# Recurrence outputs made turned by their products, and one chunk's first product moved ahead

## The chip, the cores and the metric

The kernel runs on one core of a Trainium2 chip. The metric is device time in microseconds (us) of one execution, as a median of several runs. The core has five engines that work side by side, each through its own queue in order: TensorE (PE; its weight loads are listed as PEld), VectorE (DVE), ScalarE (ACT), GpSimd (POOL), and SyncE (SP), which issues most of the transfers between device memory and the on-chip memory. TensorE writes into PSUM, eight banks of 512 words in each of 128 rows; ScalarE and VectorE read it from there.

## The reference

Two blocks follow each other. The first is a delta rule recurrence over 768 time steps for 4 batches of 8 heads of width 48, the second a gated feed-forward block over the 3072 tokens with 384 features, inner width 1536. All is in 32 bits.

```python
k_n = k / (norm(k) + 1e-6)
state = zeros((B, H, D, D))
for t in range(S):
    y[:, :, t] = einsum('bhd,bhde->bhe', q[:, :, t], state)
    v_old = einsum('bhde,bhd->bhe', state, k_n[:, :, t])
    state = state + beta[:, :, t] * einsum('bhd,bhe->bhde', k_n[:, :, t], v[:, :, t] - v_old)
x = y.transpose(0, 2, 1, 3).reshape(B * S, H * D)
g, val = x @ w_gate, x @ w_val
out = (g * sigmoid(g) * val) @ w_out
```

## The kernel before

**Recurrence.** Time is cut into 12 chunks of 64 steps. Within a chunk the loop over steps becomes matrix products, 32 small ones each (4 batches and 8 heads; the indices are `par`, the parity of the head, `j`, its pair, and `b`, `bp` for the batch). Four small matmuls with 64 rows and 64 columns work beside each other in TensorE's array. For chunk c the steps are: the **Gram products** K K' and Q K' (the second, masked, is P); the inverse of a triangular matrix made from K K' and beta, called Z, for two chunks (a group g) at a time, by substitution on blocks of 32 (`invert`, on VectorE for g = 1 and on GpSimd later) and by two **joins**; and the recurrence proper, `advance(c)`, in four stages:

1. v is scaled (`scale_v`), then K S and Q S with S the state (L1054, L1044); VectorE subtracts K S from v (L1064).
2. Z times the difference (L1073) gives u, which ScalarE copies (L1081).
3. The state gains K' u (`of_state`, L902, added by VectorE at L911); P u is added onto Q S in PSUM (L1127); three ScalarE copies take y out (L1140, L1142).
4. Six full transposes by TensorE (L1152) turn y, which has tokens in rows, into x, which has features in rows; one ScalarE copy takes it to `x_ffn` (L1153). v of the next chunk is scaled (L448).

**Feed-forward.** `x_ffn` holds one chunk, 384 features by 256 tokens, in three blocks of 128 rows. Chunks 0 and 1 are multiplied plainly (`gate_val`, L1450, and `output`, L1477). From chunk 2 on a fast scheme is used: 15 products in place of 18 for each of two rounds of gate and value (`gate_val_fast`, with every product four matmuls, at L1290), and 7 in place of 8 in the output (`output_fast`, product 1 to 7 of 6 matmuls each, L1567). Some products want sums of blocks of x (`first_x_sums`, `x_sums`), of weights (`sums_of_w`) or of the hidden values, which VectorE makes. Product 13 takes a block of x as it is, product 4 takes the fourth of the x sums. `begin(c)` issues products 4 and 13 of a chunk and their copies ahead of the rest. Chunk 2's second round is plain (`gate_val_plain`), in three pairs of blocks.

**Order.** Everything is issued in an order written out by hand. The main part of chunk c's feed-forward calls `point(c + 1)` at fixed places, which runs either a step of preparation (transposes of K and Q, Gram products, joins) or the next stage of `advance(c + 1)`; `fill(n)` runs pieces of the inverse for an estimated n us of VectorE time, and `point_and_fill` does both, with the time that the point has spent taken off n. Stage 4 writes `x_ffn`, so the point leaves it alone while `parts["x used"]` says that products still read it: it runs in `output_fast`. PSUM has four banks for the feed-forward (`ffn`), and two pairs, `px` and `py`, for the recurrence. Loads that may come late wait in `late_loads` and are issued by `load_late`.

The line numbers of the profile are those of this kernel. L1517 and L1520 are the helpers `minus` and `plus`, L1326 and L1327 the gating, L470 VectorE's transposes of K and Q, L551, L841 and L846 transposes within the inverse, L772, L781 and L797 belong to the join of group 1, L536 is the mask on P, and L525 copies parts of K K'.

## Time and profile before

| | |
|---|---|
| time, median of 3 runs | 681.98 us (680.16 to 685.14) |
| profiled execution | 681.86 us, span 680.2 us |
| mean granted clock of TensorE | 0.992 of full speed |
| TensorE busy | 657.2 us, 10850 instructions |
| VectorE busy | 474.5 us, 982 instructions |
| ScalarE busy | 255.7 us, 546 instructions |
| GpSimd busy | 197.1 us, 309 instructions |

A matmul on 32 bit data appears as two passes, so 32 small matmuls are 64 rows of the trace; a transpose is one pass. Matmuls are pipelined: the busy time of one overlaps the next, and what a group costs is better read from start to start. A wait is listed with the engine, its line and the engine and line that ended it. The timeline merges equal neighbours into a row: start, duration, engine, line, operation, out<-in, shapes, count, and in brackets the idle time before it. The recurrence of chunk c + 1 runs within the feed-forward of chunk c, from chunk 2 on in steps of some 50 us.

### The profile page before, as it was taken

The numbers are of one execution on the slowest core, as the hardware profiler recorded it, in microseconds if no ns is written. First come the engines' busy times: TensorE is split into PE (matmuls) and PEld (weight loads), VectorE is DVE, ScalarE is ACT, GpSimd is POOL, SyncE is SP. The second block draws the span as 40 slices with busy tenths as digits, with TensorE's granted clock in tenths as the row PEclk, the third lists the DMA queues.
The fourth block names the chain that finished last, engine by engine and source line by source line (L and its number), as shares of the span: only waits on it lengthen the run. The fifth ranks groups of instructions, "written<-read, shape, count | busy, mean of one in ns | idle before, by whom it ended". The sixth has DMA issues, their size and how long they took to land.

```text
span 680.2 us, 24832 instructions
## 1 busy us (share of the span) xinstructions
PE 657.2 (97%) x10850; PEld 606.2 (89%) x10850; DVE 474.5 (70%) x982; ACT 255.7 (38%) x546; POOL 197.1 (29%) x309
## 2 busy tenths in 40 slices
PE   8688999998999899999999999999999999999997
PEld 4576888756989899999999999999999999999997
DVE  6978888698579867757757847767757755646462
ACT  5777965214332342244332244332232333142130
POOL 7120032005893030882030883030883000000000
PEclk9989999999899999999999999999999999999999
DMA  9669733016136352177262177252176222132221
GB/s 135 160 191 213 224 128 105 2 37 137 41 51 159 77 124 79 46 148 150 58 137 80 38 148 153 57 116 80 26 172 140 67 86 79 41 95 78 72 77 24
DMA packets 147437, 68.56 MB, mean 101 GB/s; under 512 B 123456, under 2 KB 126560, under 8 KB 147328
## 3 DMA queue, kind: packets, MB, share of 16 engines
q1 hardware_dynamic: 144992, 66.48, 41.2%
q8 instruction: 85, 1.39, 0.8%
q10 hardware_dynamic: 2080, 0.39, 0.4%
q14 instruction: 24, 0.20, 0.1%
q0 software_dynamic: 256, 0.10, 0.1%
HBM read 59.08 MB, written 7.86 MB: 98 GB/s over the span
## 4 chain that ended last, share of the span: by engine, by line
PE 90%; DVE 6%; ACT 2%; issue 2%; DVEq 0%
PE ffn L1290 38%; PE ffn L1567 20%; PE ffn L1450 11%; PE ffn L1477 4%; PE p_px L1054 2%; PE p_px L1073 2%; PE p_py L1044 1%; PE p_px L902 1%; PE p_py L497 1%; PE p_py L1127 1%; PE p_px L497 1%; PE p_py L1152 1%; PE p_px L631 1%; PE p_px L870 1%; PE p_py L884 1%
## 5 line engine op out<-in xcount | busy, mean ns | idle before, releaser
L1290 PE MATMUL ffn<-x_t,w_gv 128*128 128x128 f32 x760 | 103.5, 280 | 2.4 <-DVE x_t L1517 1.8
L1290 PEld LDWEIGHTS ffn<-x_t,w_gv 128*128 128x128 f32 x760 | 93.1, 192 | 4.7 <-DVE x_t L1517 2.0
L1567 PE MATMUL ffn<-wo_sb,h_f 128*128 128x192 f32 x480 | 84.1, 329 | 0.0
L811 POOL TENSOR_TENSOR n_b<-mb,half 128x32 f32<-128x32 f32 x5 | 27.6, 5520 | 190.2 <-DVE mb L551 190.2
L1290 PE MATMUL ffn<-x_ffn,w_gv 128*128 128x128 f32 x600 | 81.0, 279 | 0.0
L1326 ACT ACTIVATE sil<-ffn 128x256 f32<-128x256 f32 x95 | 34.7, 383 | 118.8 <-PE ffn L1290 104.5
L1567 PEld LDWEIGHTS ffn<-wo_sb,h_f 128*128 128x128 f32 x480 | 77.8, 190 | 0.8 <-ACT ffn L1559 0.2
L580 POOL TENSOR_TENSOR h_f<-zb,mb 128x31 f32<-128x31 f32 (+15 forms) x124 | 71.0, 572 | 14.4 <-DVE mb L568 5.0
L1290 PEld LDWEIGHTS ffn<-x_ffn,w_gv 128*128 128x128 f32 x600 | 74.7, 196 | 0.0
L586 POOL TENSOR_TENSOR zb<-zb,h_f 128x31 f32<-128x31 f32 (+15 forms) x124 | 69.5, 561 | 9.7
L1290 PE MATMUL ffn<-x_t,h_f 128*128 128x128 f32 x464 | 64.2, 282 | 1.8 <-DVE ffn L1520 1.8
L1290 PEld LDWEIGHTS ffn<-x_t,h_f 128*128 128x128 f32 x464 | 56.9, 193 | 3.7 <-DVE ffn L1520 2.0
L1327 DVE TENSOR_TENSOR h_f<-sil,ffn 128x256 f32<-128x256 f32 x95 | 37.6, 418 | 22.3 <-ACT sil L1326 22.3
L1450 PE MATMUL ffn<-x_ffn,w_gv 128*128 128x256 f32 x216 | 48.0, 381 | 0.0
L1450 PEld LDWEIGHTS ffn<-x_ffn,w_gv 128*128 128x128 f32 x216 | 40.7, 190 | 5.6
L1517 DVE TENSOR_TENSOR ffn<-p_sb,ffn 128x512 f32<-128x512 f32 x36 | 25.1, 696 | 24.4 <-PE ffn L1290 23.8
L1520 DVE TENSOR_TENSOR ffn<-ffn,p_sb 128x512 f32<-128x512 f32 x36 | 24.7, 692 | 19.4 <-PE ffn L1290 16.2
L1567 PE MATMUL ffn<-last_k,h_f 128*128 128x192 f32 x200 | 35.9, 327 | 0.4 <-DVE o_sb L1520 0.4
L1450 PE MATMUL ffn<-x_t,w_gv 128*128 128x256 f32 x144 | 33.9, 385 | 0.0
L1567 PEld LDWEIGHTS ffn<-last_k,h_f 128*128 128x128 f32 x200 | 32.8, 190 | 0.7 <-DVE o_sb L1520 0.7
L1520 DVE TENSOR_TENSOR o_sb<-o_sb,ffn 128x192 f32<-128x192 f32 x49 | 16.9, 347 | 20.6 <-PE ffn L1567 20.2
L1290 PE MATMUL ffn<-x_ffn,h_f 128*128 128x128 f32 x224 | 30.3, 279 | 0.0
(343 smaller groups left out, 1168.7 us busy)
## 6 DMA issues: line engine op xcount, KB each, us to landing
h_f<-w_s SPq DMA_DIRECT2D x81, 256.0 KB, 2.7
more_w<-w_s SPq DMA_DIRECT2D x27, 256.0 KB, 2.9
vin<-in_v_dram SPq DMA_DIRECT2D x48, 96.0 KB, 3.6
out_dram<-o_sb SPq DMA_DIRECT2D x48, 96.0 KB, 2.2
kn<-in_k_dram SPq DMA_DIRECT2D x20, 192.0 KB, 4.6
w_s<-h_f SPq DMA_DIRECT2D x10, 256.0 KB, 2.3
zt<-in_moe_w_out_dram SPq DMA_DIRECT2D x6, 384.0 KB, 4.2
qpad<-in_q_dram SPq DMA_DIRECT2D x36, 64.0 KB, 3.2
```

Of the source, the lines that this page charges most:

```text
L497: nc.tensor.matmul(p_v[par][half_of(b if of_q else b ^ par), bp, j], kt[c][half_of(par), bp, j, b], xt[half_of(par), bp, j, b],)
L580: engine.tensor_tensor(out=t_v, in0=zb[:, 0 : j + 1, j : j + 1].to_broadcast([128, j + 1, m]), in1=mb[:, j : j + 1, j + 1 : R].to_broadcas ...
L586: engine.tensor_tensor(out=zb[:, 0 : j + 1, j + 1 : R], in0=zb[:, 0 : j + 1, j + 1 : R], in1=t_v, op=ALU.add,)
L811: nc.gpsimd.tensor_tensor(out=n, in0=mb.rearrange("p j i -> p (j i)")[:, 0 : R * R : R + 1], in1=half, op=ALU.pow,)
L1290: nc.tensor.matmul(p[:, u], w(u), moving, start=start and u == 0, stop=True, skip_group_check=True,)
L1326: nc.scalar.activation(silu_of, p[:, 0:2], ACTF.Silu)
L1327: nc.vector.tensor_tensor(out=h_of(c, PAIRS[r][e % 3], e // 3), in0=silu_of, in1=p[:, 2:4], op=ALU.mult)
L1450: nc.tensor.matmul(ps[name][:, i], w_sb[:, t, (f + i) * 128 : (f + i + 1) * 128], xts[c][:, t], start=(t == 0 and i == 0), stop=(t == KT - 1),
L1477: nc.tensor.matmul(p_o, hs[c, f - f % 2][:, f % 2, bp * 128 : (bp + 1) * 128], wo_sb[:, f], start=(f == 0), stop=(f == FT - 1),)
L1517: nc.vector.tensor_tensor(out=out, in0=a, in1=b, op=ALU.subtract)
L1520: nc.vector.tensor_tensor(out=out, in0=a, in1=b, op=ALU.add)
L1567: nc.tensor.matmul(p[x, part], a(f - f % 2)[:, f % 2], b(f), start=not begun and f == 0, stop=f == FH - 1, skip_group_check=True,)
```

## The change

For chunks 3 to 11 the output of the recurrence is made with features in rows at once. The state and u become the weights, Q and P the moving side, so that PSUM holds y already turned (`q_to_x`, `u_to_x`). A head has 48 features and two heads share 128 rows less than neatly, so for odd heads 64 columns are loaded as weights, the 16 before the head's own included; `state` gets 16 columns of zeros ahead for that. Half of the turned Q S stands ahead of K S in stage 1, half behind Z R in stage 2. Twelve ScalarE copies of 16 to 64 rows by 256 elements put the heads at their rows of `x_ffn` (`x_copies`); odd heads' extra rows are overwritten by later copies. Since stage 3 now writes `x_ffn`, it waits for `x used` and moves into the outputs; stage 4 keeps the scaling of v alone.

For chunk 2, K S is issued ahead of the last plain pair of chunk 1 and writes `py`; Q S follows in stage 2. For chunks 1 and 2 the state product comes after P u. `begin` of chunk 2 issues product 13 first, and that chunk's second product moves ahead of its first. Other edits change how much of the inverse is issued where (`more`, `fill`, the numbers of WAIT), and where weight sums are made.

```diff
@@ state
-    state = const.tile([128, 2, NB, NJ, D], FP32, name="state")
+    LEAD = D - R
+    state_flat = const.tile([128, LEAD + 2 * NB * NJ * D], FP32, name="state")
+    nc.gpsimd.memset(state_flat[:, 0:LEAD], 0.0)
+    state = state_flat[:, LEAD:].rearrange(
+        "p (b bp j d) -> p b bp j d", b=2, bp=NB, j=NJ
+    )
@@ invert(g)
-        for _ in range({1: 2, 2: 3}.get(g, 4)):
+        for _ in range({1: 2, 2: 1}.get(g, 4)):
             yield WAIT
...
-        yield 1 if g == 1 else 1.7
+        if g == 1:
+            scale_v(FAST)
+        yield {1: 1, 2: 2}.get(g, 1.7)
+        for _ in range(2 if g == 2 else 0):
+            yield WAIT
...
-        for _ in range(7):
+        for _ in range(6 if g == 2 else 7):
             yield WAIT
@@ new functions
+    TILES = ((0, 0), (1, 1), (0, 1), (1, 0))
+    def columns(par, at):
+        return slice(at - LEAD, at + D) if par else slice(at, at + D)
+    def q_to_x(c, p, other):
+        for bp in range(NB):
+            for x in range(2):
+                for par, half in TILES:
+                    b, j = par ^ other, 2 * x + half
+                    at = LEAD + D * (NJ * (NB * b + bp) + j)
+                    nc.tensor.matmul(
+                        p[rows_of_x(par, half), b, par, x, bp],
+                        state_flat[head_of(par), columns(par, at)],
+                        qt[c][head_of(par), bp, j, b],
+                        start=other == 1 and bp == 0 and x == 0,
...
+    def u_to_x(uu, pq, p):
+        u_of = uu.rearrange("p par bp j d -> p (par bp j d)")
...
+                        nc.tensor.matmul(
+                            p[rows_of_x(par, half), b, par, x, bp],
+                            u_of[half_of(b), columns(par, at)],
+                            pq[half_of(b), par, bp, j],
...
+    def x_copies(c, p):
+        p = p.rearrange("p b par x bp i -> p par x bp b i")
+        def copy(half, j, par, lo, rows):
+            at = D * (2 * j + par) + lo - (LEAD if par else 0)
+            nc.scalar.copy(
+                x_all[at % 128 : at % 128 + rows, at // 128].rearrange(
+                    "p (bp b i) -> p bp b i", bp=NB, b=2
+                ),
+                p[64 * half + lo : 64 * half + lo + rows, par, j // 2],
+            )
+        for half in range(2):
+            for j in (half, half + 2):
+                if j % 2:
+                    copy(half, j, 1, 0, C)
+                    copy(half, j, 0, 0, R)
+                    copy(half, j, 0, R, LEAD)
+                else:
+                    copy(half, j, 1, 0, R)
+                    copy(half, j, 1, R, R)
+                    copy(half, j, 0, 0, D)
@@ advance(c)
-        p_y = recur(ps_pair("p_y", "py"))
-        p_r = recur(ps_pair("p_r", "px"))
+        p_y = to_x("p_y") if c > FAST else recur(ps_pair("p_y", "py"))
+        p_r = p_y if c == FAST else recur(ps_pair("p_r", "px"))
...
+        if c > FAST:
+            q_to_x(c, p_y, 1)
...
-        if c > 1:
-            of_q()
...
         yield
-        if c == 1:
+        if c <= FAST:
             of_q()
...
+        if c > FAST:
+            q_to_x(c, p_y, 0)
         nc.scalar.copy(uu, p_u)
...
+        if c > FAST:
+            if c < NCH - 1:
+                of_state(c, uu)
+            u_to_x(uu, pq, p_y)
+            x_copies(c, p_y)
+            yield
+            if c < NCH - 1 and (c + 1) // 2 in n_t:
+                scale_v(c + 1)
+            yield
+            return
...
-        if c < NCH - 1:
-            of_state(c, uu)
...
+        of_state(c, uu)
@@ begin(c), gate_val_fast(c, r, fill); more at its second and third point_and_fill
+        def plain():
+            multiply(p3, 13, c, 0, True)
+            nc.scalar.copy(temps(c, 0)[0], p3)
+        if c == FAST:
+            plain()
         multiply(p4, 4, c, 0, True)
         nc.scalar.copy(p0, p4)
-        multiply(p3, 13, c, 0, True)
-        nc.scalar.copy(temps(c, 0)[0], p3)
+        if c > FAST:
+            plain()
...
+        more = 3.5 if c == FAST + 1 else 2.5
...
+        elif c == FAST:
+            multiply(p3, 2, c, r)
         multiply(p0, 1, c, r)
...
-        multiply(p3, 2, c, r)
+        if c > FAST:
+            multiply(p3, 2, c, r)
...
-        point_and_fill(c + 1, 2.5, fill)
+        point_and_fill(c + 1, more, fill)
@@ output(c, bp, fill, between), gate_val_plain
-                if (c, bp) == (1, 1):
-                    sums_of_w(0, sums_at.pop(f, ()))
+            if (c, bp) == (1, 1):
+                sums_of_w(0, sums_at.pop(f, ()))
...
-        fill(4 if c < 2 else 7)
+        fill(4)
...
-        parts["x used"] = False
         sums_of_h(c, 10)
         sums_of_w(1, (7, 8, 13))
         load_late()
         point_and_fill(c + 1, 2.5, fill)
+        parts["x used"] = False
@@ output_fast(c, fill)
             first_product()
             product_3()
+            if c + 1 < NCH and steps("advance", c + 1) < 2:
+                point(c + 1)
             fill(2)
             product_2()
...
             first_product()
+            point(c + 1)
             assert steps("advance", FAST + 1) >= 3
...
-            fill(1)
             product_3()
             plus(o[1][:, right], o[1][:, right], p[1, 0])
             x_sums(c + 1)
+            fill(1)
             point(c + 1)
...
-        fill(5)
+        if c > FAST:
+            fill(5)
@@ may_advance(c), point(c)
-        return steps("advance", c) > 0 or (c in p_sb and steps("join", g) >= due)
+        begun = steps("advance", c) > (c == FAST)
+        return begun or (c in p_sb and steps("join", g) >= due)
...
-        if steps("advance", c) == 3 and parts["x used"]:
+        if steps("advance", c) == (3 if c <= FAST else 2) and parts["x used"]:
             mine = False
@@ main part
+            if at == len(pairs) - 1:
+                step("advance", advance, FAST)
...
-        output(1, 1, fill, range(2, FT, 2))
+        output(1, 1, fill, (2, 4, 7, 9, 11))
         finish(2)
+        first_x_sums(2)
+        fill(2)
         x_sums(2)
```

More of the change, by code (lines that the diff above doesn't have):

```diff
@@ L1023, in first_advance, with to_x, rows_of_x @@
         yield
+    TILES = ((0, 0), (1, 1), (0, 1), (1, 0))
+    def to_x(name):
+        p = ps_pair(name, "py")
+        return p.rearrange("p b (par x bp i) -> p b par x bp i", par=2, x=2, bp=NB)
+    def columns(par, at):
+        return slice(at - LEAD, at + D) if par else slice(at, at + D)
+    def rows_of_x(par, half):
+        return half_of(half) if par else head_of(half)
+    def q_to_x(c, p, other):
[9 more added lines that the diff above has]
+                        start=other == 1 and bp == 0 and x == 0,
+                        stop=False,
+                        skip_group_check=True,
+                    )
@@ new lines, in u_to_x @@
+    def u_to_x(uu, pq, p):
+        u_of = uu.rearrange("p par bp j d -> p (par bp j d)")
+        for bp in range(NB):
+            for par in range(2):
+                for x in range(2):
+                    for b, half in TILES:
+                        j = 2 * x + half
+                        at = D * (NJ * (NB * par + bp) + j)
+                        nc.tensor.matmul(
+                            p[rows_of_x(par, half), b, par, x, bp],
+                            u_of[half_of(b), columns(par, at)],
+                            pq[half_of(b), par, bp, j],
+                            start=False,
+                            stop=True,
+                            skip_group_check=True,
+                        )
@@ new lines, in x_copies @@
+    def x_copies(c, p):
+        p = p.rearrange("p b par x bp i -> p par x bp b i")
+        xts[c] = x_all
+        def copy(half, j, par, lo, rows):
[5 more added lines that the diff above has]
+                p[64 * half + lo : 64 * half + lo + rows, par, j // 2],
+            )
+        for half in range(2):
[8 more added lines that the diff above has]
+                    copy(half, j, 0, 0, D)
@@ L1153, in advance @@
         nc.scalar.copy(xts[c].rearrange("p t (bp n) -> p t bp n", bp=NB), p_f)
-        if 2 <= c < NCH - 1 and (c + 1) // 2 in n_t:
+        if c == FAST and (c + 1) // 2 in n_t:
             scale_v(c + 1)
@@ L1392, in gate_val_fast @@
             sums_of_h(c, 8)
-        point_and_fill(c + 1, 2.5, fill)
+        point_and_fill(c + 1, more, fill)
         def last():
@@ L1887 @@
         zb_1 = work.tile([128, R, R], FP32, name="zb", bufs=1)
-        new_nt(0, spare_of_q, state.rearrange("p b bp j d -> p (b bp j d)")[:, 0:512])
+        new_nt(0, spare_of_q, state_flat[:, LEAD : LEAD + 512])
         new_nt(1, zb_1.rearrange("p k i -> p (k i)"), spare_of_q[:, 0:512])
```

## The prediction

> **What bounds the kernel now.** I read the page's busy times and the chain that ended last first, then TensorE's list of waits, then its timeline around each wait.
>
> ```profile
> PE 657.2 (97%) x10850; PEld 606.2 (89%) x10850; DVE 474.5 (70%) x982; ACT 255.7 (38%) x546; POOL 197.1 (29%) x309
> ...
> PE 90%; DVE 6%; ACT 2%; issue 2%; DVEq 0%
> ```
>
> TensorE is busy for 97% of the span and carries 90% of the chain, so a microsecond taken off it is gained unless another engine is late just there. The list of its waits (total us, times, longest) has these as the long ones after the first 80 us:
>
> ```profile
> PE ffn L1290 <- DVE x_t L1517: 1.8, 1, 1.8
> PE ffn L1290 <- DVE ffn L1520: 1.8, 1, 1.8
> ...
> PE ffn L1567 <- DVE o_sb L1520: 0.4, 1, 0.4
> ```
>
> All three lie round chunk 2. The first, in the timeline (start, us, instructions, idle before):
>
> ```profile
> 170.13 1.70 PE L1290 MATMUL ffn<-x_t,w_gv 128*128 128x128 f32 x8 [1.84 <-DVE x_t L1517]
> 171.62 1.91 PE L1290 MATMUL ffn<-x_ffn,w_gv 128*128 128x128 f32 x8
> 173.32 1.38 PE L1290 MATMUL ffn<-x_ffn,h_f 128*128 128x128 f32 x8
> 174.54 1.06 PE L1290 MATMUL ffn<-x_t,w_gv 128*128 128x128 f32 x8
> ```
>
> The row after these starts 0.89 later, the usual step of such a product. The three products after the wait take 1.49, 1.70 and 1.22, together 1.74 too long, and the table of stretches (length, busy times, then granted clock, DMA share, GB/s) says why:
>
> ```profile
> 172.00:174.00 2.00, 2.00 (x12) 2.00 (x11) 1.46 (x2) 0.86 (x2) 1.76 (x4) 0.50 0.00 0
> ...
> 236.00:239.00 3.00, 3.00 (x16) 3.00 (x16) 0.42 (x1) 0.59 (x1) 0.00 (x0) 0.53 0.90 107
> ```
>
> The granted clock halves after an idle time of 1.8. So each wait costs about 3.55 (1.84+1.74; the second, before 235.06, costs 1.81 plus 0.68, 0.82 and 0.24). A wait of 1.34 near 64 us was followed by full clock, so the threshold lies between 1.34 and 1.81. [...]
>
> **Transposes removed.** One steady chunk on TensorE:
>
> ```profile
> 426.53 2.11 PE L1567 MATMUL ffn<-last_k,h_f 128*128 128x192 f32 x12
> 428.48 0.82 PE L1152 MATMUL p_py<-ident,y 128*128 128x128 f32 x6
> 429.13 4.07 PE L1567 MATMUL ffn<-wo_sb,h_f 128*128 128x192 f32 x24
> 433.04 1.46 PE L1567 MATMUL ffn<-last_k,h_f 128*128 128x192 f32 x8
> ```
>
> From start to start the output products take 1.95 each (24 passes: 3.91), so the six transposes cost 429.13-428.48 = 0.65. The changed kernel's built order has them for chunks 1 and 2 only. Nine groups go; chunk 3's is hidden (below), which leaves 8 x 0.65 = **5.2 saved**.
>
> **The turned products.** Q S and P U keep 32 matmuls each. What was 48 columns moving over 64 columns of weights becomes 64 moving over weights of 48 (first heads of each pair) or 64. Starts in the timeline give K S 0.97 (64 weight columns, 48 moving, 396.61 to 397.58), a Gram product 0.98 (64 and 64, 419.47 to 420.45) and the state product 0.76 (48 and 48, 409.05 to 409.81). So widening the moving side to 64 costs 0.01, and narrowing both is worth 0.21. No row has 48 weight columns and 64 moving, so a group lies between 0.76 and 0.98 against 0.97 now: over 2 x 8 groups, from 0.2 lost to 3.4 gained. The Gram row is nearest, as it has the 64 moving; I take **0.3**. [...] The number of switches between small and full products per chunk stays, so the 0.1 seen on each side of a small group is not counted.
>
> **Twelve ScalarE copies** take the place of three into y (0.48, 0.47, 0.47) and one into x:
>
> ```profile
> L525 ACT COPY a_sb<-p_px 32x256 f32<-32x256 f32 x32 | 11.6, 362 | 0.7
> L1153 ACT COPY x_ffn<-p_py 128x768 f32<-128x768 f32 x11 | 8.8, 797 | 20.1 <-PE p_py L1152 20.1
> ```
>
> Each copies 256 elements per row from PSUM; the row of that size says 0.36, so 4.35 instead of 2.22 per chunk. From below, the 192-element copy out of PSUM (0.32) gives 3.8; from above, the slowest 256-element copy, with strided reads (0.63), gives 7.6. I take 0.36. ScalarE has room, but x comes later. Let T be the end of the turned P U, now in the output stage with the state product (both moved there from the gate stage, at no change of TensorE's work). Products 4, 5, 6 and 7 follow, so the next chunk begins at T+7.8. The copies end at T+4.6. VectorE meanwhile waits for product 5 (T+3.9), adds it (0.3), scales v (0.9, to T+5.1) and only then makes the four sums that the first gate product wants (1.3, to T+6.4). So x sums wait for VectorE, not for the copies: hidden, with 1.4 to spare, and covered until a copy takes 0.5. A second chain is thinner: product 6's sum, six more x sums (1.7), product 7's sum, then the copy (0.57) that frees the bank of the third gate product. From product 5's end it adds to 5.6 against 5.8 on TensorE. Of this margin of 0.2 I charge **0.5** in all, between 0 and 2.4 (0.3 in each of 8 chunks).
>
> **Chunk 2 earlier.** K S ahead of the last plain pair costs the same 0.97 there; its subtraction and the scaling of v (0.9 each) fall before a VectorE idle time of 3.10 at 123.5, so the inverse behind them is not later. It uses the bank of the y products, free by then. In the outputs Q S then stands one block after the joining copies (ScalarE, 2.34 after 155.3, to 157.83), and must wait for them about 0.3, as 157.88 shows now. From 155.3, in times of the old trace: Q S 157.9, Z R 158.9, two output matmuls 161.5, P U and state 163.4, two matmuls 164.9, transposes 165.5, one matmul 166.3, joins 167.0. Then the first gate product is the plain one, which needs no sums (x is there at 166.5). Sums are done by 167.9, TensorE reaches them at 168.0. ScalarE's queue (output copy, two joining copies, one scaling, 2.2 from 166.5) holds product 2 about 0.3. The second join starts near 172.1 instead of 176.4; less the 1.07 that K S now takes ahead of this stretch, **3.2 saved**. If the old wait stays whole: 0.
>
> **Chunk 3's begin.** In the output of chunk 2 VectorE is the bound: it has no idle time from 210 to 236.
>
> ```profile
> 226.73 1.24 DVE L470 STREAM_TRANSPOSE kn<-qpad 128x1024 f32<-128x1024 f32 x1
> 227.89 1.20 DVE L470 STREAM_TRANSPOSE qt<-qpad 128x1024 f32<-128x1024 f32 x1
> ...
> 231.56 1.54 DVE L846 STREAM_TRANSPOSE z<-zt 32x256 f32<-32x256 f32 x4
> ...
> 234.32 1.29 DVE L1520 TENSOR_TENSOR ffn<-ffn,p_sb 128x512 f32<-128x512 f32 x2
> ```
>
> The same VectorE work stands before the transposes of K and Q in both orders, so the Gram products still start at 228.0 and 229.15; TensorE, 0.65 and the old 0.4 wait earlier, now idles about 1.2 there, below the threshold. What goes is the inverse work between 229.5 and 233.1, moved behind the two sums at 234.32. The sums then end about 234.7 (ScalarE's Gram copies, done at 233.4, set that) and product 7 starts at 232.95 instead of 235.06. The moved half transpose and two smaller ones (1.9) then delay the subtraction that the fifth product wants: to 237.2, a new wait of about 1.5, against 239.47 now. **2.2 saved**; without the new wait 3.8, and 0.5 if 1.5 of idle time also slows the clock (1.74).
>
> At nothing: the memset of 16 columns on GpSimd early (its 0.4 idle ahead of the powers covers it), the state product after P U in chunks 1 and 2, the changed places of weight sums, and the loads of K and v (SP's order keeps them within the same chunk; no wait for a DMA is on TensorE's list after the start).
>
> **Sum.** 5.2 + 0.3 - 0.5 + 3.2 + 2.2 = 10.4. The profiled execution took 681.86 (span 680.2 and 1.7 around it), 0.1 under the median of 681.98. **Predicted: 671.5**, or 1.5% less. About 1% (6.8 us) is what a measurement of this kernel can tell from no change.
>
> **Rivals.**
> - *A restart stays.* One of the two waits at chunks 2 and 3 persists or is replaced by one of over 1.5, so that half of their 5.4 is left, and the thin margins cost 2.4: 5.2 - 2.4 + 2.7 = 5.5, so about **676.5**. For: VectorE stays the bound at 210 to 230, and both new margins there are under 0.3. Against: most of each 3.55 is the slow clock, which a shorter wait avoids.
> - *Everything pays.* The turned groups lie halfway between the two rows (0.87, worth 1.6) and no new wait comes: 5.2 + 1.6 + 3.2 + 3.8 = 14, so **668**. Against: 1.9 of VectorE work has to fit in 1.0.
> - *x too late in every chunk: slower.* At 0.68 a copy the twelve end at T+8.3 and the sums at T+9.6, a wait of 1.8 at each begin. From there the clock drops too: 9 x 3.55 = 32, so about **703**. Up to 0.65 it is only 9 x 1.4 = 13, no faster and no slower than now. Against: 0.36 to 0.42 in every row of 256 elements out of PSUM; only strided reads reach 0.63, and these copies read runs of 64.
> - *It doesn't do it.* Excluded: the built order has the turned products in nine chunks and 54 transposes fewer.
>
> **How the numbers follow.** Forecast (668.5 to 675) 0.60; a restart stays (675 to 680) 0.22; everything pays (665 to 668.5) 0.10; slower 0.05; gains eaten by short waits (680 to 688) 0.03. Below 675.2 lie the forecast, "everything pays" and a little of the first rival: faster 0.72, same 0.23, slower 0.05. The range 666 to 679 leaves out under two in ten.
>
> **What would show it.** Only 12 transposes into x left; ScalarE groups of 32, 48, 64 and 16 x 256 near 0.36; the waits of 1.84 and 1.81 gone, with full clock at 170 to 176; a wait near 1.2 at chunk 4's Gram product and near 1.5 on the subtraction after; no wait on x sums after 240 us; the steady chunks (50 us each: 277.87 to 428.48 for three) shorter by 0.6. I am wrong if the turned groups take over 1.1, if the copies take over 0.5, or if a new wait exceeds 1.8.

## The result, and the profile after

The changed kernel takes 677.07 us (median of 11 runs, 673.63 to 680.25), the kernel before 681.36 beside it (11 runs, 678.41 to 685.83). The ratio is **0.9931, 95% interval 0.9907 to 0.9954**: 4.7 us gained (3.1 to 6.3), where 10.4 were forecast. The profiled execution took 675.77, span 674.1, so it lies 1.3 under its median; against the span before it is 6.1 shorter. Twelve transposes into x are left, as forecast, and twelve copies per chunk take their place. From the page's busy times and its groups (busy us, mean ns):

```profile
PE 648.0 (96%) x10796; PEld 596.9 (89%) x10796; DVE 475.9 (71%) x982; ACT 275.3 (41%) x618; POOL 199.5 (30%) x310
...
L1084 ACT COPY x_ffn<-p_py 32x256 f32<-32x256 f32 (+3 forms) x108 | 39.3, 364 | 36.6 <-PE p_py L1069 34.9
```

Where the six transposes of a chunk stood between output products, the turned P U now stands, 1.03 from start to start (timeline, start and us):

```profile
269.57 0.94 PE L911 MATMUL p_px<-uu,kn 64*48 64x48 f32 x64
270.32 1.10 PE L1069 MATMUL p_py<-p_sb,uu 64*48 64x64 f32 x64
271.35 4.17 PE L1666 MATMUL ffn<-wo_sb,h_f 128*128 128x192 f32 x24
```

Line numbers are now those of the changed kernel: L1378 (before L1290) is the fast products' helper, L1666 (L1567) that of the output, L1616 and L1619 (L1517, L1520) `minus` and `plus`, L879 and L893 (L870, L884) the two joins, L502 (L497) the Gram products, L475 (L470) the transposes of K and Q.

TensorE's list of waits (total us, times, longest) after the start:

```profile
PE p_px L879 <- issue: 2.0, 2, 1.0
PE ffn L1666 <- DVE last_k L1616: 1.9, 1, 1.9
PE ffn L1378 <- DVE p_sb L1616: 1.8, 4, 1.2
...
PE p_px L502 <- DVE kn L475: 0.9, 1, 0.9
```

Both waits of 1.8 with the slow clock behind them are gone: from 46 us to TensorE's last product this profile has no half clock. The two waits that the forecast announced have come, 0.87 at chunk 4's Gram products (about 1.2 forecast) and 1.22 on the subtraction behind them (about 1.5; the longest of the four on `p_sb`). Not forecast are 1.93 on weight sums (`last_k`) in chunk 2's output and two of 0.99 and 0.98 at joins, where nothing that the profile shows was waited for; the kernel before had one of those, of 0.55.

The same points of both traces, in us from the span's start, with the forecast's shift summed up to each:

| point | before | after | shift | forecast |
|---|---|---|---|---|
| second join of group 1, start | 176.42 | 173.03 | -3.4 | -3.2 |
| Gram products of chunk 4, start | 228.03 | 227.26 | -0.8 | -3.2 |
| fifth product of chunk 3, first round | 239.47 | 236.40 | -3.1 | -5.4 |
| first gate product of chunk 4 | 282.43 | 279.25 | -3.2 | -6.0 |
| first gate product of chunk 11 | 634.36 | 628.52 | -5.8 | -10.4 |
| end of span | 680.2 | 674.1 | -6.1 | -10.4 |

So two stretches fell short: chunk 2's output (2.3 us by its fifth product), and the seven steps from chunk 4's begin to chunk 11's (351.93 to 349.27, 2.7 us in place of 4.4). A smaller loss lies between them: a new wait of 0.47 on VectorE in chunk 3's first round, at 242.72.

### The profile page after: what moved, and what is told of

It reads as the page before. It is cut to its first block, busy times and chain, and to the rows that moved or that the text cites. A ratio compares the mean times of both kernels' runs of the same rounds, so it can differ in the third digit from the quotient of the medians.

```text
span 674.1 us, 24788 instructions
## 1 busy us (share of the span) xinstructions
PE 648.0 (96%) x10796; PEld 596.9 (89%) x10796; DVE 475.9 (71%) x982; ACT 275.3 (41%) x618; POOL 199.5 (30%) x310
## 3 DMA queue, kind: packets, MB, share of 16 engines
q8 instruction: 85, 1.39, 0.9%
## 4 chain that ended last, share of the span: by engine, by line
PE 62%; DVE 3%; ACT 1%; issue 1%; DVEq 0%; ACTq 0%
PE ffn L1378 35%; PE ffn L1666 19%; PE p_py L1052 1%; PE p_px L1150 1%; PE p_py L1069 1%; PE p_px L1133 1%; PE p_py L502 1%; PE p_px L911 1%; PE p_px L879 1%; PE p_py L893 1%; PE p_px L502 1%; DVE zt L897 1%; ACT zt L897 0%; DVE p_sb L1616 0%; DVE o_sb L1619 0%
## 5 line engine op out<-in xcount | busy, mean ns | idle before, releaser
L1378 PE MATMUL ffn<-x_t,w_gv 128*128 128x128 f32 x760 | 103.0, 279 | 2.3 <-DVE p_sb L1616 1.8
L1378 PEld LDWEIGHTS ffn<-x_t,w_gv 128*128 128x128 f32 x760 | 92.7, 192 | 4.8 <-DVE p_sb L1616 2.6
L1666 PE MATMUL ffn<-wo_sb,h_f 128*128 128x192 f32 x480 | 84.3, 329 | 0.0
L1378 PE MATMUL ffn<-x_ffn,w_gv 128*128 128x128 f32 x600 | 79.5, 275 | 0.1
L1666 PEld LDWEIGHTS ffn<-wo_sb,h_f 128*128 128x128 f32 x480 | 77.9, 190 | 0.9
L591 POOL TENSOR_TENSOR zb<-zb,h_f 128x31 f32<-128x31 f32 (+15 forms) x124 | 72.3, 583 | 9.7
L1378 PEld LDWEIGHTS ffn<-x_ffn,w_gv 128*128 128x128 f32 x600 | 73.0, 192 | 0.4 <-ACT last_h L1424 0.3
L1378 PE MATMUL ffn<-x_t,h_f 128*128 128x128 f32 x464 | 63.6, 280 | 0.0
L1378 PEld LDWEIGHTS ffn<-x_t,h_f 128*128 128x128 f32 x464 | 56.3, 192 | 1.8 <-DVE ffn L1616 0.9
L1084 ACT COPY x_ffn<-p_py 32x256 f32<-32x256 f32 (+3 forms) x108 | 39.3, 364 | 36.6 <-PE p_py L1069 34.9
L1549 PEld LDWEIGHTS ffn<-x_ffn,w_gv 128*128 128x128 f32 x216 | 40.7, 190 | 5.6
L1616 DVE TENSOR_TENSOR ffn<-p_sb,ffn 128x512 f32<-128x512 f32 x36 | 25.0, 696 | 24.4 <-PE ffn L1378 23.8
L1619 DVE TENSOR_TENSOR o_sb<-o_sb,ffn 128x192 f32<-128x192 f32 x49 | 17.0, 349 | 30.8 <-PE ffn L1666 30.4
L1666 PE MATMUL ffn<-last_k,h_f 128*128 128x192 f32 x200 | 36.1, 328 | 2.1 <-DVE last_k L1616 1.9
L1619 DVE TENSOR_TENSOR ffn<-ffn,p_sb 128x512 f32<-128x512 f32 x36 | 24.7, 690 | 15.4 <-PE ffn L1378 13.6
L1666 PEld LDWEIGHTS ffn<-last_k,h_f 128*128 128x128 f32 x200 | 32.9, 190 | 2.8 <-DVE last_k L1616 2.2
```

Source lines behind the costliest of these rows:

```text
L591: engine.tensor_tensor(out=zb[:, 0 : j + 1, j + 1 : R], in0=zb[:, 0 : j + 1, j + 1 : R], in1=t_v, op=ALU.add,)
L1084: nc.scalar.copy(x_all[at % 128 : at % 128 + rows, at // 128].rearrange("p (bp b i) -> p bp b i", bp=NB, b=2), p[64 * half + lo : 64 * hal ...
L1378: nc.tensor.matmul(p[:, u], w(u), moving, start=start and u == 0, stop=True, skip_group_check=True,)
L1549: nc.tensor.matmul(ps[name][:, i], w_sb[:, t, (f + i) * 128 : (f + i + 1) * 128], xts[c][:, t], start=(t == 0 and i == 0), stop=(t == KT - 1),
L1616: nc.vector.tensor_tensor(out=out, in0=a, in1=b, op=ALU.subtract)
L1619: nc.vector.tensor_tensor(out=out, in0=a, in1=b, op=ALU.add)
```

## Experiments

### The two halves of the change

Turned products alone: the changed kernel with the chunk 2 edits, the first outputs' and the sums' order put back.

```diff
-        p_r = p_y if c == FAST else recur(ps_pair("p_r", "px"))
+        p_r = recur(ps_pair("p_r", "px"))
...
-        if c > FAST:
-            fill(5)
+        fill(5)
```

> The changed kernel with every edit for chunk 2, the first outputs and the order of sums undone: only chunks 3 to 11 have the turned products and the twelve ScalarE copies. By the prediction's sum it saves 5.2 + 0.3 - 0.5 = 5.0 us against the kernel before (about 676.4 against 681.4). By my reading of the two traces (six steady chunks lost 2.0 us instead of 3.9, because the join's products after the Gram products found TensorE waiting for nothing the profile shows) it saves less: nine steps of 0.34, about 3.0, so about 678.4. If the loss at the joins came from the places that the chunk 2 edits gave the stages, this kernel would save the full 5.0 and show no issue waits of about 1 us at the join's products; if it comes from the turned order itself, they are here too. The two waits of 1.84 and 1.81 before the first gate products of chunks 2 and 3 should stay, each with the granted clock at about half behind it.

Chunk 2's edits alone: the turned products put back to transposes.

```diff
-        p_y = to_x("p_y") if c > FAST else recur(ps_pair("p_y", "py"))
+        p_y = recur(ps_pair("p_y", "py"))
...
-        if c > FAST:
-            if c < NCH - 1:
-                of_state(c, uu)
-            u_to_x(uu, pq, p_y)
-            x_copies(c, p_y)
```

> The changed kernel with the turned products undone: chunks 3 to 11 transpose y as before, only the edits for chunk 2, the outputs and the order of sums are in. By the prediction's sum it saves 3.2 + 2.2 = 5.4 us against the kernel before. By my theory that VectorE, slowed by GpSimd's substitution for group 2, takes back in chunk 2 what its earlier start had gained, it saves about 2.5 to 3, with the second join of group 1 ending 3.4 earlier and the fifth product of chunk 2's output only about 3 earlier. VectorE's operations of 512 elements with two on-chip inputs should take 0.85 to 1.1 between 195 and 212 us, as they do in the changed kernel. If the new waits in chunk 2 came from the turned products and their copies instead, the wait of 1.9 before product 2 of chunk 2's output would be gone here and the saving would be 5.4.

Measured: turned alone 0.9963 (0.9924 to 1.0003), chunk 2 alone **1.0055 (1.0015 to 1.0094)**, so about half a per cent longer. In the first, the second joins of chunks 4 and 6 waited 2.18 and 0.91, and a product waited 1.08 for a load; chunk 4 to chunk 11 took 350.80 in place of 351.93. Without these three waits it would be 346.6, which is what the turned products would make of the stretch. So waits at joins don't need the chunk 2 edits. They don't need the turned order either: chunk 2's edits alone have one of 1.04. That these edits alone lose time was not foreseen; 2.5 to 3 us of gain were expected. The two halves do not add up: alone they make -0.4% and +0.6%, together -0.7%. TensorE's timeline of chunk 2's edits alone shows what was lost (start, us, instructions, idle before):

```profile
284.73 1.81 PE L1369 MATMUL ffn<-x_t,w_gv 128*128 128x128 f32 x8 [3.22 <-DVE x_t L1607]
```

The sums of x of chunk 4 came 3.2 late, and the granted clock was 0.50 from 285.1 to 288.4. The joins of chunk 4 stood six products (24 matmuls; the expectation below calls these products) later than before, at 249.8 in place of 245.2, and the recurrence with its four stages behind them. One edit does that: pieces of the inverse, an estimated 5 us of VectorE's time, that chunk 2's output no longer issues at its end. So it alone was put back:

```diff
-        if c > FAST:
-            fill(5)
+        fill(5)
```

> As e2_chunk2_alone (turned products undone), with one more edit undone: 5 us of the inverse of group 2 are issued again at the end of chunk 2's output, ahead of chunk 3. In e2_chunk2_alone the joins of chunk 4 stood 24 products later than in the kernel before (start 249.8 against 245.2), the recurrence of chunk 4 with its four stages followed them, and its first sums of x came 3.2 us late, with the clock at half behind. Theory, coupling: that edit, which the prediction counted as a gain at chunk 3's begin, takes the lead away that four stages need; turned, three stages are left and it costs nothing. Then here the wait of 3.2 and the slow clock behind it go and the time falls by 4 to 5 us against e2_chunk2_alone, to the kernel before's or 1 to 2 under it. Rival: x is late because K S and Q S themselves are slower or the copies into y are; then the wait stays above 2.

Measured: 0.9984 (0.9952 to 1.0016), 0.7% under the kernel that it was made from. Chunk 4 begins at 280.75 without a wait, and its first join stands at 243.18. The coupling holds: the edit costs the lead that four stages need. The turned order, with three, doesn't need it: in the changed kernel the first join stands at 248.31, nearly as late as with chunk 2's edits alone (249.8), and chunk 4 begins without a wait. The waits on `last_k` (1.39 and 0.97) are in both of these kernels, so they don't come from the turned products.

### Chunk 2: VectorE beside GpSimd

In the changed kernel's VectorE timeline, while GpSimd substitutes for group 2 (to 214.35):

```profile
195.18 1.10 DVE L1616 TENSOR_TENSOR more_w<-w_gv 128x512 f32<-128x512 f32 x1
196.31 1.08 DVE L1616 TENSOR_TENSOR h_f<-more_w,w_gv 128x512 f32<-128x512 f32 x1
...
198.33 0.94 DVE L1141 TENSOR_TENSOR vin<-vin,p_px 128x768 f32<-128x768 f32 x1
199.19 1.60 DVE L1616 TENSOR_TENSOR last_h<-wo_sb 128x1152 f32<-128x1152 f32 x1
...
214.68 1.35 DVE L1616 TENSOR_TENSOR last_k<-wo_sb 128x1152 f32<-128x1152 f32 x1
```

Sums of 512 elements take 1.1 here, sums of 1152 take 1.60 with GpSimd at work and 1.35 after it. The kernel before shows the same kind of lengths, while GpSimd works there (to 211.45):

```profile
198.46 1.08 DVE L1517 TENSOR_TENSOR more_w<-w_gv 128x512 f32<-128x512 f32 x1
...
202.27 1.41 DVE L1517 TENSOR_TENSOR last_h<-wo_sb 128x1152 f32<-128x1152 f32 x1
...
215.50 1.35 DVE L1517 TENSOR_TENSOR last_k<-wo_sb 128x1152 f32<-128x1152 f32 x1
```

What differs is how long the two engines run beside each other. VectorE now comes to this work 3.4 earlier, while GpSimd starts at 170.33 (before: 168.07) and ends 2.9 later, since the masked part that it waits for is now made behind the first sums of x. VectorE's timeline lists no idle time from 196.61 on in the kernel before, and none from 193.22 on in the changed one; from there to the first sum for `last_k` the same operations take 18.89 before and 21.46 after, so 2.57 of the 3.4 are lost. The next kernel leaves out GpSimd's substitution for group 2, so part of that inverse is not computed:

```diff
-        for _ in substitute(mb, zb, nc.gpsimd):
-            pass
+        if g > 2:
+            for _ in substitute(mb, zb, nc.gpsimd):
+                pass
```

> The changed kernel with GpSimd's substitution for group 2 (chunks 4 and 5) left out: 31 steps of GpSimd between 170 and 214 us are not done, so part of that inverse is not computed; all else is issued as in the changed kernel. Theory, contention: VectorE's operations of 512 elements with two on-chip inputs take 0.68 instead of 0.85 to 1.1 between 195 and 212 us, the wait of 1.93 on the weight sums before product 2 of chunk 2's output goes, the Gram product's wait of 0.87 goes or moves, and the fifth product of that output starts 2 to 3 us earlier; 2 to 3 us off the whole. Rival, amount of work: VectorE simply has too much to do in that stretch whoever else runs; then its operations keep their lengths, the wait of 1.93 stays within 0.5, and the time changes by less than 0.5.

The same operations in its timeline:

```profile
192.62 0.69 DVE L1617 TENSOR_TENSOR more_w<-w_gv 128x512 f32<-128x512 f32 x1
193.34 0.69 DVE L1617 TENSOR_TENSOR h_f<-more_w,w_gv 128x512 f32<-128x512 f32 x1
...
194.56 0.94 DVE L1142 TENSOR_TENSOR vin<-vin,p_px 128x768 f32<-128x768 f32 x1
195.42 1.35 DVE L1617 TENSOR_TENSOR last_h<-wo_sb 128x1152 f32<-128x1152 f32 x1
```

0.69 and 1.35; the subtraction that reads PSUM takes 0.94 in both. The same row of operations now takes 18.02 with 1.88 of idle time in it. The wait on `last_k` is gone. From the first fast product to the fifth of chunk 3's first round it takes 64.95 in place of 68.45, so 3.5 less (ratio to the kernel before 0.9878, 0.9814 to 0.9943). Contention between the two engines holds; the rival, which wanted unchanged lengths, falls.

Three moves take the load off without leaving work out: GpSimd's masked part first, the state's sum behind the sum that product 2 wants, and three weight sums later.

```diff
+        fill(2)
         first_x_sums(2)
-        fill(2)
...
-            nc.vector.tensor_tensor(out=state, in0=state, in1=p_s, op=ALU.add)
+            def add():
+                nc.vector.tensor_tensor(out=state, in0=state, in1=p_s, op=ALU.add)
+            deferred.append(add) if c == 3 else add()
...
             combos.pop(0)()
+            deferred.pop()()
...
-            sums_of_w(1, (3, 9, 10))
```

The last goes into chunk 3's first round.

> The changed kernel with three moves in chunk 2: (1) the masked parts of group 2 that GpSimd's substitution waits for are made ahead of the first sums of x instead of after them, so that GpSimd starts and ends about 2 us earlier; (2) VectorE adds the state product of chunk 3 after the weight sums for product 2 instead of ahead of them; (3) two weight sums for other products wait until chunk 3. If VectorE's amount and slowness in the stretch 195 to 236 us set the end of chunk 2's output, the wait of 1.93 before product 2 shrinks by 1.0 or more and the whole is 1.5 to 3 us shorter than the changed kernel. If VectorE's queue only hides another bound (the late start of the Gram products, held by the transposes of K and Q), the wait shrinks but the fifth product starts where it did, and the time stays within 0.5 of the changed kernel.

Measured: 0.9856 (0.9799 to 0.9913). The wait on `last_k` is gone, the Gram products wait 0.27, and the stretch takes 65.57, 2.9 less. The first move alone, then the other two alone:

> The changed kernel with the first of the three moves alone: GpSimd's substitution for group 2 starts about 2 us earlier. If its running beside VectorE is what costs, VectorE works 2 us less beside it (512 elements in about 1.0 in place of 0.68, so 0.6 us) and makes 0.8 of the masked parts in a time when it had been idle (166.7 to 167.5): the wait of 1.93 before product 2 shrinks to about 0.6 and the fifth product of chunk 2's output comes about 1.3 us earlier against the first fast product (68.45 in the changed kernel). If only VectorE's order near the end counts, the wait stays above 1.5.

> The changed kernel with the other two moves alone: the state of chunk 3 is added behind the weight sum that product 2 wants (0.94 us out of its way), and two... three weight sums (1.88 us) are made in chunk 3 in place of ahead of the transposes of K and Q. By the amount of VectorE's work the wait of 1.93 shrinks to about 1.0, the Gram product's wait of 0.87 goes, and the fifth product comes 1.9 us earlier against the first fast product. With the first move's 1.3 that is 3.2 for all three; e4_order showed 2.9. If the transposes of K and Q were bound by something other than VectorE's queue, the fifth product moves by less than 0.5.

| | stretch, us | against 68.45 | expected | wait on `last_k` | ratio to before |
|---|---|---|---|---|---|
| first move | 67.06 | -1.4 | -1.3 | 0.83 | 0.9893 (0.9851 to 0.9934) |
| other two | 66.58 | -1.9 | -1.9 | 1.10 | 0.9891 (0.9852 to 0.9930) |
| all three | 65.57 | -2.9 | | none | 0.9856 (0.9799 to 0.9913) |

Both kinds of move shorten the stretch. The second is the amount of work that stands in VectorE's queue ahead of product 2 and of the transposes of K and Q. The first mixes two things, which the expectation puts at 0.6 for less work beside GpSimd and 0.8 for masked parts made while VectorE had been idle; only the kernel without the substitution shows contention by itself. The stretch repeats well enough for this: 68.45, 68.47 and 68.45 in three kernels with the changed order, 64.89 to 65.83 in the six with all three moves.

### The joins: TensorE's instructions

The first join of chunk 4 in the changed kernel's timeline, and the instruction queue on its page (packets, MB, share):

```profile
343.19 1.27 PE L879 MATMUL p_px<-zt,a_sb 32*32 32x32 f32 x126
345.46 0.22 PE L879 MATMUL p_px<-zt,a_sb 32*32 32x32 f32 x2 [0.99 <-issue]
```

```profile
q8 instruction: 85, 1.39, 0.9%
```

A join is 128 matmuls in 1.2 us; this one stops after 126. 1.39 MB in 85 packets is 16 KB each; TensorE's some 21,600 instructions (matmuls and weight loads) over 85 are 254 to a packet. Counted in the trace, 3584 of TensorE's instructions (1779 matmuls, 1779 loads, 26 of its sequencer) lie between the ends of this kernel's two waits at joins, 345.46 and 447.00, which is 14 x 256; in the kernel before, 256 (128 matmuls, 128 loads) lie between the issue waits that end at 32.61 and 37.16. So the theory: instructions come in blocks of 256, 128 matmuls with their loads, and a join uses up a block faster than the next arrives. In all kernels here the waits of over 0.3 at joins that the profile puts down to nothing stand behind 105 to 127 of the 128 matmuls (0.55 behind 108 in the kernel before), and none behind fewer. Tiny unread products at the start shift the edges: 18 (36 matmuls, as each appears twice), or 64, which is a whole block.

```diff
+    def small_unread(count, p):
+        for n in range(count):
+            rows = slice(R * (n % 4), R * (n % 4) + R)
+            nc.tensor.matmul(p[rows, 0:16], half[rows], half[rows, 0:16])
...
         unread(3, p_unread)
+        small_unread(18, p_unread)
```

> The kernel with the three moves in chunk 2 (e4_order) plus 18 tiny products of 32 by 32 by 16 that nobody reads, issued by TensorE in its first microseconds while it waits for loads: 36 matmuls with their weight loads, so 72 instructions. Theory, instruction supply: TensorE's instructions arrive in blocks of 256 (85 packets and 1.39 MB on their queue, 16 KB each), and a join of 128 small matmuls uses up a block in 1.27 us. In e4_order the waits stood behind 126 and 105 matmuls of a join (1.27 us and 1.37, the granted clock at half for some 2 us behind the first), in the kernel before behind 108 (0.55), and none where the edge of a block fell at 87 or less. With 36 matmuls ahead the edges of chunks 4 and 6 fall at 90 and 69: both waits go, and the granted clock stays full, so the profile is 3 to 4.5 us shorter after 325 us than e4_order's; a wait of up to 1 us may come at chunk 2's join, whose edge moves to 111. Rival, collision with the loads of K and Q that run at that place: then 72 instructions elsewhere change nothing, the waits stay behind about the same time of day, at 1 us or more, and the time is that of e4_order.

> As e5_order_shift18 with 64 such products: 128 matmuls, 256 instructions, just one block. By the theory of instruction supply the edges come back to where they were, and with them the two waits of 1.3 us at the joins of chunks 4 and 6 (behind about 126 and 105 matmuls) and the slow clock; time as e4_order within 1 us (the 64 products themselves take under 2 us, beside the first loads). If merely more instructions ahead were the cause, the waits would move or go here even more than with 18.

With all three moves and no shift, then with 64:

```profile
340.38 1.27 PE L880 MATMUL p_px<-zt,a_sb 32*32 32x32 f32 x126
342.91 0.22 PE L880 MATMUL p_px<-zt,a_sb 32*32 32x32 f32 x2 [1.27 <-issue]
```

```profile
342.15 1.27 PE L886 MATMUL p_px<-zt,a_sb 32*32 32x32 f32 x126
344.58 0.22 PE L886 MATMUL p_px<-zt,a_sb 32*32 32x32 f32 x2 [1.16 <-issue]
```

With 64 the edges are back at 126 and, in chunk 6, at 105 (1.15). The queue of that kernel agrees, with one packet more:

```profile
q8 instruction: 86, 1.41, 0.9%
```

With 18 both waits are gone, and one of 1.12 has come behind 127 matmuls of chunk 8's second join. The theory holds in its places. The whole times don't show a gain: 0.9901 (0.9864 to 0.9938) with 18 and 0.9894 (0.9849 to 0.9940) with 64, against 0.9856 (0.9799 to 0.9913) for the three moves alone; the intervals overlap. From chunk 4's begin to chunk 11's the kernel with 18 takes 349.69 in place of 351.60. With 18, edges fell on other dense places (issue waits of 0.95 at 27.1, 1.03 at 32.2, 0.93 at 167.7), and behind chunk 4's second join a product waited 1.76 for a load. The same 18 on the changed kernel and on the turned products alone:

> The changed kernel with the same 18 products. By instruction supply its two waits of 0.99 and 0.98 at the joins of chunks 4 and 6 go: 2.0 us less after 325 us, all else as in the changed kernel, so about 0.3% faster than it. By the rival (collision with loads alone) they stay and the time is the changed kernel's.

> The turned products alone (e1_turned_alone) with the same 18 products. There the second join of chunks 4 and 6 waited 2.18 and 0.91. By instruction supply these go (edges at 90 and 69), and what is left is the price of the turned products themselves: by the prediction 5.0 us less than the kernel before, so 0.7% faster, and without the waits of the kernel before (0.55) up to 5.5. If the turned products are worth less for another reason (their groups of 1.02 to 1.07 in place of 0.97, thin margins), it stays at e1_turned_alone's 0.4%, with no waits at the joins.

0.9980 (0.9953 to 1.0007) and 0.9980 (0.9950 to 1.0010): neither gained, against expectation. The first lies above the changed kernel's 0.9931 with intervals that barely touch, the second can't be told from the 0.9963 without the 18. In the first the joins of chunks 4 and 6 don't wait, but a load costs 1.88 at 356.82, and issue waits of 0.3 to 1.6 stand at eight places of the first 170 us (in the changed kernel at three). In the second the edges simply fell elsewhere in joins (2.15 behind 123 matmuls, 0.65 behind 111). So the shift was placed behind all that, ahead of chunk 4, with 15 products:

```diff
+        if c == FAST + 2:
+            small_unread(15, p4)
         multiply(p4, 4, c, 0, True)
```

> The three moves of e4_order, with 15 tiny unread products ahead of chunk 4's first gate product (near 276 us) in place of the 18 at the very start, so that nothing before that place changes. By instruction supply the edges of blocks in the first joins of chunks 4 and 6 move from 126 and 105 to 96 and 75: the waits of 1.27 and 1.37 fall to under 0.6 in all, and the slow clock behind the first goes. What then decides is the load of weights behind them: in e5_order_shift18, where those waits were gone, the fourth product after chunk 4's second join waited 1.8 for a load from device memory that SyncE had issued behind eight loads of Q. If that load is the next bound, a wait of 1 to 2 us on it appears here and the time is e4_order's within 1.5 us; if it was only late there because the early part ran differently, the time falls by 3 to 4 us.

Its timeline at chunk 4, TensorE, then SyncE's issues:

```profile
339.27 1.29 PE L886 MATMUL p_px<-zt,a_sb 32*32 32x32 f32 x128
...
346.05 1.29 PE L900 MATMUL p_py<-t,z 32*32 32x32 f32 x128
348.31 0.91 PE L1387 MATMUL ffn<-x_t,h_f 128*128 128x128 f32 x6 [0.98 <-DMA h_f<-w_s]
```

```profile
340.07 5.16 SPq L172 DMA_DIRECT2D qpad<-in_q_dram  x8
345.33 0.43 SPq L1306 DMA_DIRECT2D h_f<-w_s  x1
```

No join waits; the next bound is the load of weights that SyncE issues only at 345.33, behind a row of eight loads of Q that takes it 5.16. The stretch from chunk 4's begin to chunk 11's is 348.41, where the three moves had 351.6 (two waits of 1.27 and 1.37, and 1.7 for 3.4 us of half clock behind the first). Ratio 0.9884 (0.9841 to 0.9926). The rows were then cut in half, without and with the shift:

```diff
-                late_loads.append(lambda: load_blocks(of_q, c + 1))
+                late_loads.append(lambda: load_blocks(of_q, c + 1, (0,)))
+                late_loads.append(lambda: load_blocks(of_q, c + 1, (1,)))
```

> The three moves of e4_order; besides, the eight loads of a chunk's K and the eight of its Q that SyncE issues in a row (4 to 5 us each, near 335 and 340 us) are issued in two halves of four, at two of the places where such late loads are issued. TensorE's instructions are in the same places as in e4_order. If the instruction blocks come late because the transfers are crowded there (DMA share 0.99 at 344 to 346 us in the changed kernel), the waits behind 126 and 105 matmuls of the joins shrink from 1.27 and 1.37 to under 0.7; if a block takes as long anyway, they stay within 0.3. No load of weights should be waited for.

> The three moves of e4_order with both: 15 unread products ahead of chunk 4 and the loads of K and Q in halves. If edges of instruction blocks and SyncE's row of loads are what took the gain near 340 to 352 us, there is neither an issue wait over 0.6 at the joins of chunks 4 and 6 nor a wait for weights, and the time is 3 to 4 us under e4_order's, near 668 to 670. If one of them only hid a third bound, that one shows up here as a new wait at chunk 4 or 6.

With halves alone the wait behind 126 grew to 1.99, though the transfers there were thinner (DMA share 0.55 from 342 to 344, against 0.82 from 344 to 346 in the changed kernel):

```profile
341.47 1.27 PE L881 MATMUL p_px<-zt,a_sb 32*32 32x32 f32 x126
344.73 0.21 PE L881 MATMUL p_px<-zt,a_sb 32*32 32x32 f32 x2 [1.99 <-issue]
```

The expectation's 0.99 for the changed kernel is 0.82 in the table, and 0.98 from 343 to 344. The wait should have shrunk to under 0.7 if crowded transfers made the blocks late; it grew, which speaks against collision, by one profile. Ratio 0.9897 (0.9846 to 0.9948). With both, neither wait is left, chunk 4 to chunk 11 takes **347.02**, and the ratio is 0.9863 (0.9812 to 0.9915). Last, both on the changed kernel as it is:

> The changed kernel with its order in chunk 2 as it is; only the 15 unread products ahead of chunk 4 and the loads of K and Q in halves are added. If the edges of instruction blocks alone took the missing part of the turned products' gain, the waits of 0.99 and 0.98 at the joins go, no load of weights is waited for, and the stretch from the first gate product of chunk 4 to that of chunk 11 takes 347.0 as in e12_order_both (changed kernel 349.3, kernel before 352.0): 2.3 us less, ratio to the kernel before near 0.990. If the stretch depends on how early chunk 2 ends, it stays over 348.5.

347.27 in place of 349.27, and 0.9903 (0.9866 to 0.9940), as expected. No join waits. Chunk 2's stretch stays at 68.45 there, so the two losses are independent.

The six kernels with the three moves lie between 0.9856 and 0.9901, so clear of the kernel before and 0.3% to 0.8% under the changed kernel's 0.9931. All their intervals reach into its own (0.9907 to 0.9954), so that part is probable and not shown by the times; which of the six is best they can't tell either. The trace speaks for the one with shift and halves, which has no wait left at the joins and the shortest stretch there.

## Why the prediction was wrong

The sign and most mechanisms were right, the size was not: 10.4 forecast, 4.7 measured. Point by point, by the prediction's steps:

- **Transposes, 8 x 0.65: right price, not all of it collected.** Seven steps from chunk 4 to chunk 11 should give 7 x 0.62 = 4.4 (5.2 + 0.3 - 0.5 = 5.0 for eight). They gave 2.7. Without waits at joins they gave 4.9 and 4.7 (347.02 and 347.27 against 351.93), of which 0.55 is a wait that the kernel before had too. So the sum holds, and what was missing in it is a term for TensorE's own instructions: 0.99 + 0.98 - 0.55 = 1.4 of the missing 1.7. The sign of it stood in the list of waits before, an "issue" of 0.55 at a join; the prediction has no step for it.
- **Turned groups, 0.3 gained: nothing.** Q S in two halves and P U take 2.11 from start to start (chunk 4's feed-forward), before 2.10. The Gram row was the right one to choose, but by that row alone (0.98 against 0.97) 0.2 would have been lost; the 0.3 gained leaned towards the state row. No run shows the group of 0.87, worth 1.6, that "everything pays" adds up: the loads themselves take 120 ns with 48 columns and 135 with 64, but the groups did not become shorter by it.
- **Twelve copies at 0.36:** 364 ns, right; no steady chunk waits for sums of x. The rival "x too late in every chunk" falls.
- **Chunk 2 earlier, 3.2: right** up to the second join (3.4), with the wait of 0.3 before Q S at 0.39. That the two numbers lie so close owes something to luck: counted from the transposes of K at 68.40 before and 69.01 after, behind the uneven start, the join comes 4.0 earlier.
- **Chunk 3's begin, 2.2: here the sum failed.** It was worked out in times of the old trace, "the Gram products still start at 228.0", and added to the 3.2, as though VectorE's work had come 3.2 earlier along with TensorE's. The Gram products came 0.8 earlier. From there to the fifth product the forecast 2.2 was collected (2.3, by the two waits that it named), so what got lost is most of the 3.2. The step that failed is "the same VectorE work stands before the transposes of K and Q in both orders": it is the same work, but it was priced at its old length. VectorE's queue is full from 196.61 on in the old trace already (the prediction looked from 210 on). Come 3.4 earlier, that work stands beside GpSimd for longer, which itself ends at 214.35 in place of 211.45, and it takes 21.46 in place of 18.89. Of 5.4 for both steps 3.1 was left; moving that work gave 2.9 back.
- **The rival "a restart stays"** had the time (676.5), half by luck. One part of its condition came, a new wait of over 1.5 (1.93 on `last_k`, which is also over the 1.8 that the prediction named as a sign of being wrong). But no slow clock followed, and the 2.4 that it charged for thin margins was not lost. Its remark that most of each 3.55 is the slow clock is not right either, as that part is 1.74. The nearest was "VectorE stays the bound at 210 to 230" among its reasons.
- **A dependence that the sum leaves out: the places of the inverse.** With four stages, the moved pieces of the inverse at the end of chunk 2's output cost 0.7% (chunk 2's edits alone against the same with this undone). The edit is bearable only because the other half of the change shortens the recurrence to three stages; the prediction priced the parts as if they were independent.
- **The threshold of the clock, "between 1.34 and 1.81": wrong** as a rule for a wait by itself, see below. It did no harm to the sum here, as no wait after the start of the changed kernel slowed the clock.

The profile's 6.1 lies 1.4 above the 4.7 of the ratio. Single executions differ that much: among profiles of kernels with the changed start and nothing added to it, the first fast product comes between 164.55 and 169.75, with issue waits and waits for K of different lengths in the first 70 us. The mean granted clock of the changed kernel's executions lies between 0.987 and 0.994, too. Stretches from a fixed point, as used above, are free of that.

## What to carry to other kernels

Before a gain found on one engine is added to a gain found further on, ask whether every engine that bounds the second place moves with the first; a full queue does not. Price an operation beside the neighbour that will run with it: VectorE's sums with both inputs in on-chip memory were up to 2.1 times as long while GpSimd worked (0.88 for 0.42 with 256 elements, 1.1 for 0.69 with 512, 1.60 for 1.35 with 1152). Where TensorE runs hundreds of tiny matmuls in a row, count the instructions between its "issue" waits. In the kernels before and after those of over 0.2 stood whole blocks of 256 apart, give or take one instruction; 15 unread products ahead of chunk 4 took away those at the joins: the 1.27 and 1.37 of the three moves and, with the loads in halves too, the 0.99 and 0.98 of the changed kernel. 18 at the start brought one of 1.12 to another join.

## What the runs showed of the hardware

**Instruction blocks.** TensorE waited 0.55 to 2.18 us at joins where 105 or more of the 128 small matmuls stood ahead of an edge. Blocks of 256 instructions rest on the counts between waits (14 x 256 and 256), and the 85 packets of 16 KB, the 86 with 256 instructions more and the shift by a whole block agree with them. How far ahead a block is asked for, no record shows.

**GpSimd and VectorE.** Only sums with both inputs in on-chip memory were slowed (0.69 to 1.1); with one input in PSUM they kept 0.94. What it is that the two engines contend for, no record shows.

**The clock.** In these traces half clock (0.50 granted) came in pieces of 3.41 us, on a grid: in the kernel before from 170.57 to 173.98 and from 235.42 to 238.84, 64.85 or 19.0 pieces apart; with halves alone the two starts are 102.40 or 30.0 pieces apart (read from tables of short stretches). The wait of 1.27 behind a join's 126 small matmuls, with the three moves, was followed by half clock (0.50 from 344.11 on), the wait of 1.93 in the changed kernel by full clock, as its table of stretches shows (length, busy times of the engines, then granted clock, DMA share, GB/s):

```profile
216.10:219.50 3.40, 3.40 (x21) 3.40 (x22) 3.40 (x7) 0.00 (x0) 0.00 (x0) 1.00 0.97 252
```

So no threshold for the length of a wait by itself fits these traces. How it falls on the grid and what else lies in its piece may count. In the kernel before the wait of 1.84, from 168.29 to 170.13, lies whole in the piece of 3.41 before 170.57, where half clock starts. What share of a piece decides is open. By the grid of the changed kernel's profile (half clock from 38.45 to 45.27) about 1.8 of the wait of 1.93 lie in one piece, and the clock stayed full; with the turned products alone a wait of 1.69 within one piece did the same, while 1.81 in the kernel before was followed by half clock.
